# Holding K and V pools open across the dense phases of a decode step with gradients, with early V loads, fewer weight slabs and smaller K and V pools

## The chip, the cores and the metric

The kernel runs on one core of one Trainium2 chip. The metric is the time of one execution on the device in microseconds (us), as the median of several runs. A kernel that is compared is timed on the same chip, in the same rounds, as the kernel before. Ratios are the mean time of one kernel's fast runs over that of the other's fast runs of the same rounds, so they are not quite the ratio of the medians quoted beside them. Ratios are turned into microseconds with 2180 us.

## The reference, cut to what matters

Two layers of grouped-query attention over a cache of 65536 positions, and two feed-forward layers, for a single token, with all gradients. Both attention layers use the same K and V cache, and both feed-forward layers the same weights.

```python
def _A_ref(x, k_cache, v_cache, wq, wo):       # 32 query heads, 4 KV heads, head size 128
    q = (x @ wq)...
    scores = einsum("bhqd,bhkd->bhqk", q, k) * Dh ** -0.5
    o = einsum("bhqk,bhkd->bhqd", softmax(scores), v)
    return o... @ wo
x = A_x
x = x + _A_ref(_layernorm(x), ...)             # attention 1
x = x + _B_ref(_layernorm(x), w1, b1, w2, b2)  # relu(.)**2 in between
x = x + _A_ref(_layernorm(x), ...)             # attention 2
x = x + _B_ref(_layernorm(x), ...)
# outputs: x and its vjp: dx, dk_cache, dv_cache, dwq, dwo, dw1, db1, dw2, db2
```

## The kernel before

K and V are 67 MB each. They are read four times: by the two forward attentions, by a third pass that finds the query gradient of the second layer, and by a fourth pass that finds the rest and writes the gradients of both caches. Between the passes lie dense phases that read the weights. A border between a pass and a dense phase is called a seam below.

Every load goes through one queue, that of SP. A block of K or V is 512 KB, a weight slab 1 MB (896 KB of `w1`). Each attention opens its own pool of 8 K and 8 V blocks (4 and 4 in the fourth); each dense phase opens a pool of 6 slabs, and closes it at its end.

```python
KVBUFS = 8
...
@with_exitstack
def dense_phase(dctx, fn, resident_elems=0, wbufs=6):
    DENSE["w"] = dctx.enter_context(tc.tile_pool(name="wpool", bufs=wbufs))
    ...
    return fn()
...
class Stream:
    def block8(self, g, c8):
        ...
        if self.cur != (g, bb):
            self.t = ATT["kv"].tile([P, self.nblk, J, DH], BF, name=self.tag, tag=self.tag)
            self.eng.dma_start(out=self.t[:], in_=...)
        return self.t[:, bi, j:j + 8, :]
...
def attn_fwd(actx, qT, eT, lname):
    ...
    ATT["kv"] = actx.enter_context(tc.tile_pool(name=lname + "_kv", bufs=KVBUFS))
    ktpool = actx.enter_context(tc.tile_pool(name=lname + "_kt", bufs=5))
    spool = actx.enter_context(tc.tile_pool(name=lname + "_sp", bufs=2))
    ...
    # kT transposes K, kS forms scores; v8 (P times V) runs 78 items of 8 x 128 positions later
    pipeline(NI, [(kT, 0), (kS, TLEAD), (v8, TLEAD + IPG + LAG8)])
```

The last line gives each forward attention three stretches: one that reads K alone (the first 78 of 256 items), one where K and V alternate, and one that reads V alone (the last 78).

The row dots of the backward pass (`RowDots`, used by `mv_T`) multiply each row of a weight slab by a vector, shared out to DVE, ACT and PE. In the tail, `mv_T` over `wq` is interleaved with background tiles of the gradient of `wq` (`bg_per_block`).

## Time and profile before

| | before |
|---|---|
| time, median | 2180.55 us (2178.66 to 2184.33) |
| profiled span | 2176.8 us |
| bytes moved | 825.57 MB, mean 379 GB/s |

Lines of the page of the kernel before: the span, then the DMA row and the rate in 40 equal slices (9 is 90% or more busy), and the DMA total.

```profile
span 2176.8 us, 69255 instructions
DMA  8999999999999999699999987899999999999976
GB/s 350 388 407 408 406 398 358 401 353 390 407 407 405 390 365 392 250 407 408 407 406 404 388 340 245 316 415 405 353 417 418 393 409 393 407 410 416 412 291 235
DMA packets 229106, 825.57 MB, mean 379 GB/s; under 512 B 23748, under 2 KB 23748, under 8 KB 223684
```

The rate is 404 to 408 GB/s in the slices where the first three passes stream K and V steadily, up to 418 in the fourth, and lower at the seams. Next, the table of stretches of the kernel before, cut at the stages that the timeline of PE shows. The columns are the stretch in us, its length, busy time and count on PE, PE's weight load, DVE, ACT and POOL, the granted clock, the DMA share and GB/s. The lines are, in order: K alone in attention 1, K and V in attention 1, the dense phase between attentions 1 and 2, then K alone, K and V, and V alone in attention 2, the third attention, and the row dots before the fourth.

```profile
26.80:91.80 65.00, 56.01 (x1223) 54.74 (x1222) 39.77 (x68) 36.64 (x53) 0.00 (x0) 1.00 0.99 382
91.80:317.80 226.00, 192.59 (x4316) 177.41 (x4315) 96.41 (x162) 89.63 (x125) 0.00 (x0) 0.98 1.03 406
...
367.80:454.70 86.90, 45.87 (x1170) 43.40 (x1169) 24.91 (x68) 18.92 (x34) 0.00 (x0) 0.50 0.95 364
454.70:519.80 65.10, 58.20 (x1256) 57.01 (x1255) 42.38 (x72) 34.50 (x52) 0.00 (x0) 0.92 0.98 382
519.80:746.10 226.30, 190.80 (x4284) 173.55 (x4283) 95.26 (x161) 88.61 (x124) 0.00 (x0) 1.00 1.03 406
746.10:795.70 49.60, 36.83 (x631) 31.87 (x629) 2.25 (x10) 7.52 (x19) 0.00 (x0) 0.62 0.95 369
...
916.60:1254.40 337.80, 289.38 (x6184) 249.35 (x6184) 137.68 (x197) 111.84 (x111) 0.00 (x0) 0.98 1.01 400
1254.40:1366.40 112.00, 68.02 (x862) 59.58 (x862) 90.83 (x176) 79.21 (x97) 3.54 (x2) 0.54 0.78 283
```

The issues of the SP queue before, from its timeline (start, length from the first to the last of the group, tile, count):

```profile
431.70 13.94 SPq L268 DMA_DIRECT2D w_slab<-in_A_wq_dram  x5
454.78 51.84 SPq L401 DMA_DIRECT2D kblk<-in_A_k_cache_dram  x40
506.67 0.64 SPq L401 DMA_DIRECT2D vblk<-in_A_v_cache_dram  x1
...
795.68 1.49 SPq L268 DMA_DIRECT2D w_slab<-in_A_wo_dram  x3
...
916.00 2.95 SPq L401 DMA_DIRECT2D vblk<-in_A_v_cache_dram  x6
```

Each first load after a seam is issued only when the earlier pool is wholly free: K at 454.78 us when the last product with `wq` ends, `wo` at 795.68 us when the last V product ends, V at 916.00 us after the last row dot.

### The profile page before, as it was taken

The numbers are of one execution on the slowest core, as the hardware profiler recorded it, in microseconds if no ns is written. First come the engines' busy times: TensorE is split into PE (matmuls) and PEld (weight loads), VectorE is DVE, ScalarE is ACT, GpSimd is POOL, SyncE is SP. The second block draws the span as 40 slices with busy tenths as digits, with TensorE's granted clock in tenths as the row PEclk, the third lists the DMA queues.
The fourth block names the chain that finished last, engine by engine and source line by source line (L and its number), as shares of the span: only waits on it lengthen the run. The fifth ranks groups of instructions, "written<-read, shape, count | busy, mean of one in ns | idle before, by whom it ended". The sixth has DMA issues, their size and how long they took to land. (4 is left out here: it accounts for less than half of the span.)

```text
span 2176.8 us, 69255 instructions
## 1 busy us (share of the span) xinstructions
PE 1696.0 (78%) x30344; PEld 1332.2 (61%) x30344; DVE 1202.5 (55%) x2148; ACT 1002.1 (46%) x1532; POOL 280.4 (13%) x524
## 2 busy tenths in 40 slices
PE   5988876579888754688888866787887888788875
PEld 5978775578777744577777755444554444455542
DVE  4644430345434302744434478877877877776776
ACT  2543440235433300633333367566566566665644
POOL 0000000000000000000000000333433433443320
PEclk9999995579999955599999955899999999998976
DMA  8999999999999999699999987899999999999976
GB/s 350 388 407 408 406 398 358 401 353 390 407 407 405 390 365 392 250 407 408 407 406 404 388 340 245 316 415 405 353 417 418 393 409 393 407 410 416 412 291 235
DMA packets 229106, 825.57 MB, mean 379 GB/s; under 512 B 23748, under 2 KB 23748, under 8 KB 223684
## 3 DMA queue, kind: packets, MB, share of 16 engines
q1 hardware_dynamic: 184836, 655.46, 76.9%
q0 software_dynamic: 43968, 165.70, 18.9%
q8 instruction: 237, 3.88, 0.7%
q14 instruction: 65, 0.53, 0.1%
HBM read 655.37 MB, written 165.69 MB: 377 GB/s over the span
## 5 line engine op out<-in xcount | busy, mean ns | idle before, releaser
L175 DVE COPY kt<-ps_tr 128x1024 bf16<-128x1024 bf16 x482 | 331.4, 688 | 264.5 <-PE ps_tr L438 131.8
L172 ACT CAST gst<-ps_gg 128x512 bf16<-128x512 f32 x607 | 323.8, 593 | 187.1 <-PE ps_gg L768 139.7
L175 DVE CAST gst<-ps_gg 128x512 bf16<-128x512 f32 x417 | 273.2, 685 | 82.7 <-PE ps_gg L768 55.1
L172 ACT COPY kt<-ps_tr 128x1024 bf16<-128x1024 bf16 x158 | 159.8, 1012 | 307.7 <-PE ps_tr L438 143.0
L175 DVE COPY kt<-ps_gr 128x1024 bf16<-128x1024 bf16 x245 | 168.2, 687 | 164.7 <-PE ps_gr L438 90.6
L438 PEld LDWEIGHTS <-kblk 128*128 128x128 bf16 x4096 | 239.1, 99 | 16.8 <-issue 10.5
L457 PE MATMUL ps_sc<-L_qpad,kt 128*128 128x64 bf16 x4096 | 201.6, 195 | 57.1 <-DVE kt L175 48.6
L172 ACT COPY kt<-ps_gr 128x1024 bf16<-128x1024 bf16 x139 | 140.7, 1012 | 210.7 <-PE ps_gr L438 115.6
L768 PE MATMUL ps_gg<-GG,xt 64*128 64x512 bf16 x1024 | 193.2, 394 | 44.9 <-ACT og L172 19.1
L702 PEld LDWEIGHTS <-vblk 128*128 128x128 bf16 x2048 | 138.4, 101 | 138.0 <-issue 124.5
L501 PE MATMUL ps_acc<-eT,vblk 128*128 128x64 bf16 x4096 | 198.4, 206 | 24.0 <-DMA vblk<-in_A_v_cache_dram 22.5
L457 PEld LDWEIGHTS <-kt 128*128 128x128 bf16 x4096 | 159.3, 99 | 82.2 <-DVE kt L175 68.0
L501 PEld LDWEIGHTS <-vblk 128*128 128x128 bf16 x4096 | 169.7, 104 | 37.0 <-DMA vblk<-in_A_v_cache_dram 35.4
L702 PE MATMUL ps_tr<-ident_b,vblk 128*128 128x128 bf16 x2048 | 183.8, 227 | 6.5 <-ACT xt L172 5.8
L350 ACT ACTIVATE junka<-mvt_t 128x1024 bf16<-128x1024 bf16 (+2 forms) x88 | 139.9, 1590 | 96.1 <-DMA w_slab<-in_B_w_dram 59.3
L791 POOL MEMSET gw_ar<- 128x3584 bf16 (+1 forms) x2 | 4.1, 2052 | 1361.1 <-DVE mvt_t L349 1361.1
L438 PE MATMUL ps_tr<-ident_b,kblk 128*128 128x128 bf16 x2048 | 160.8, 222 | 12.7 <-DMA kblk<-in_A_k_cache_dram 9.3
L438 PE MATMUL ps_gr<-ident_b,kblk 128*128 128x128 bf16 x2048 | 159.7, 222 | 0.0
L603 PEld LDWEIGHTS <-vblk 128*128 128x128 bf16 x2048 | 118.1, 99 | 19.1 <-DMA vblk<-in_A_v_cache_dram 13.6
L762 PE MATMUL ps_acc<-X,kblk 128*128 128x64 bf16 x2048 | 118.9, 196 | 0.0
L172 ACT CAST og<-ps_gg 128x512 bf16<-128x512 f32 x139 | 81.1, 585 | 81.9 <-DMA out_dram<-og 44.1
L626 PE MATMUL ps_sc<-B_dOpad,kt 128*128 128x64 bf16 x2048 | 98.4, 195 | 26.0 <-DVE kt L175 19.9
(222 smaller groups left out, 2397.9 us busy)
## 6 DMA issues: line engine op xcount, KB each, us to landing
kblk<-in_A_k_cache_dram SPq DMA_DIRECT2D x512, 512.0 KB, 10.2
vblk<-in_A_v_cache_dram SPq DMA_DIRECT2D x512, 512.0 KB, 10.1
out_dram<-gst POOLq DMA_DIRECT2D x256, 512.0 KB, 10.5
w_slab<-in_A_wq_dram SPq DMA_DIRECT2D x32, 1024.0 KB, 8.2
w_slab<-in_A_wo_dram SPq DMA_DIRECT2D x32, 1024.0 KB, 12.7
w_slab<-in_B_w_dram SPq DMA_DIRECT2D x32, 896.0 KB, 8.3
w_slab<-in_B_w_dram SPq DMA_DIRECT2D x21, 1024.0 KB, 13.8
out_dram<-og POOLq DMA_DIRECT2D x60, 256.0 KB, 8.6
```

The source lines that it names most:

```text
L172: nc.scalar.copy(out=out, in_=in_)
L175: nc.vector.tensor_copy(out=out, in_=in_)
L350: nc.scalar.activation(out=self.junka[:, 0:N], in_=t[:, 0:N], func=ACTF.Copy, accum_out=self.y[:, kc:kc + 1])
L438: nc.tensor.transpose(pt[:, i, :], kb8[:, i, :], ident_b[:, :])
L457: nc.tensor.matmul(ps_s[:, slot:slot + 8, :].rearrange("p a b -> p (a b)"), lhsT=kt[:, i, :], rhs=qpad[:, g, :, :].rearrange("p a b -> p ( ...
L501: nc.tensor.matmul(ps_o[:, :, :].rearrange("p a b -> p (a b)"), lhsT=vb8[:, i, :], rhs=eT[:, g, :, c:c + 8], start=(c == 0), stop=(c == C ...
L603: nc.tensor.transpose(pt[:, i, :], vb8[:, i, :], ident_b[:, :])
L626: nc.tensor.matmul(ps_dp[:, slot:slot + 8, :].rearrange("p a b -> p (a b)"), lhsT=vt[:, i, :], rhs=dOpad[:, g, :, :].rearrange("p a b -> p ...
L702: nc.tensor.transpose(pt[:, i, :], vb8[:, i, :], ident_b[:, :])
L762: nc.tensor.matmul(ps_dq[:, :, :].rearrange("p a b -> p (a b)"), lhsT=kb8[:, i, :], rhs=X[:, sl:sl + 2, :].rearrange("p a b -> p (a b)"), ...
L768: nc.tensor.matmul(pgs[t2][:, :], lhsT=xt[64 * t2:64 * t2 + 64, blk0 + half, :], rhs=GG[64 * t2:64 * t2 + 64, :, :, :].rearrange("p a b c ...
L791: nc.gpsimd.memset(rows[:, 0:n], 0.0)
```

## The change

The intent: let loads cross the seams. For the first three attentions the K and V pool is opened before the dense phase, so the first blocks can be loaded while it runs. To make room, this pool has 4+4 instead of 8+8 buffers in the second and third attention (the fourth had 4+4 before), and the dense phases have 4 slabs instead of 6. In each forward attention up to six V blocks are asked for early, during the K-only stretch. The tail gets 8 instead of 4 background tiles per block. Arithmetic and traffic stay the same. The diff, with cuts:

```diff
+    VPRE = 6
+    KVBUFS_G = 4
...
-    def dense_phase(dctx, fn, resident_elems=0, wbufs=6):
+    def dense_phase(dctx, fn, resident_elems=0, wbufs=4):
...
+        def prefetch(self, g, bb):
+            ...
+            self.pre[(g, bb)] = self._load(g, bb)
...
-        ATT["kv"] = actx.enter_context(tc.tile_pool(name=lname + "_kv", bufs=KVBUFS))
+        assert ATT.get("kv") is not None
...
         def kT(idx):
             g, c8 = items[idx]
             kb8 = kstream.block8(g, c8)
+            if g == 0 and NPRE > 0:
+                step = max(1, (IPG - 8) // NPRE)
+                if idx % step == step - 1 and idx // step < NPRE:
+                    vstream.prefetch(0, idx // step)
...
+    kvs = open_kv("kv1", KVBUFS)
     L1 = dense_phase(lambda: attn_q(x0, "L1"))
     L1["oT"], L1["oTb"], L1["rZ"] = attn_fwd(L1["qT"], eT1, "L1")
+    kvs.close()
+    kvs = open_kv("kv2", KVBUFS_G)
...                                    # likewise kv3 (4+4) before the third attention
-            dn1 = mv_T(A_wq, D, QD, dqT1[:], "B1_dn", bgtasks=wq_tasks, bg_per_block=4)
+            dn1 = mv_T(A_wq, D, QD, dqT1[:], "B1_dn", bgtasks=wq_tasks, bg_per_block=8)
```

More of the change, by code (lines that the diff above doesn't have):

```diff
@@ L394, in __init__, with _load @@
             self.nblk = nblk
+        def _load(self, g, bb):
+            t = ATT["kv"].tile([P, self.nblk, J, DH], BF, name=self.tag, tag=self.tag)
+            self.eng.dma_start(out=t[:], in_=self.views[g][bb * self.nblk:(bb + 1) * self.nblk].rearrange("n p j d -> p n j d"))
+            return t
+        def prefetch(self, g, bb):
+            if not hasattr(self, "pre"):
+                self.pre = {}
+            self.pre[(g, bb)] = self._load(g, bb)
         def block8(self, g, c8):
@@ L399, in block8 @@
             if self.cur != (g, bb):
-                self.t = ATT["kv"].tile([P, self.nblk, J, DH], BF, name=self.tag, tag=self.tag)
-                self.eng.dma_start(out=self.t[:], in_=self.views[g][bb * self.nblk:(bb + 1) * self.nblk].rearrange("n p j d -> p n j d"))
+                pre = getattr(self, "pre", {})
+                if (g, bb) in pre:
+                    self.t = pre.pop((g, bb))
+                else:
+                    self.t = self._load(g, bb)
                 self.cur = (g, bb)
@@ L431, in attn_fwd @@
         state = {}
+        NPRE = min(VPRE, C // J)
         def kT(idx):
@@ L587, in attn_bwd3 @@
         state = {}
-        ATT["kv"] = ctx3.enter_context(tc.tile_pool(name=lname + "_kv", bufs=KVBUFS))
+        assert ATT.get("kv") is not None
         ktpool = ctx3.enter_context(tc.tile_pool(name=lname + "_kt", bufs=5))
@@ L659, in attn_bwd4 @@
         dqT = vec.tile([P, HQ], F32, name=lname + "_dqT")
-        ATT["kv"] = ctx4.enter_context(tc.tile_pool(name=lname + "_kv", bufs=4))
+        assert ATT.get("kv") is not None
         ktpool = ctx4.enter_context(tc.tile_pool(name=lname + "_kt", bufs=3))
@@ L820, in outer2_tasks, with open_kv @@
                 yield unit
+    def open_kv(name, bufs):
+        st = ExitStack()
+        ATT["kv"] = st.enter_context(tc.tile_pool(name=name, bufs=bufs))
+        return st
+    kvs = open_kv("kv1", KVBUFS)
     L1 = dense_phase(lambda: attn_q(x0, "L1"))
     L1["oT"], L1["oTb"], L1["rZ"] = attn_fwd(L1["qT"], eT1, "L1")
+    kvs.close()
+    kvs = open_kv("kv2", KVBUFS_G)
     def g12():
@@ L832 @@
     L3["oT"], L3["oTb"], L3["rZ"] = attn_fwd(L3["qT"], eT3, "L3")
+    kvs.close()
+    kvs = open_kv("kv3", KVBUFS_G)
     def g23():
@@ L842 @@
     dqT3 = attn_bwd3(L3, dOT3, nd23, eT3, "B3")
+    kvs.close()
     def g34():
@@ L882, in bg @@
                     t()
+        kvs = open_kv("kv4", 4)
         dqT1 = attn_bwd4(L1, L3, dOT1, dOT3, nd21, nd23, eT1, eT3, "B1", bg=(bg if BGON else None))
+        ATT["kv"] = None
+        kvs.close()
         for t in tasks:
```

## The prediction

> **What bounds the kernel now.** DMA. The page's DMA row stands at 9 in nearly all slices; the table of stretches shows 405-408 GB/s where K and V stream steadily, up to 418 in the last backward pass. 825.57 MB at 407 GB/s take about 2028 us; the span is 2176.8 us. (The Trainium skill, "DMA: Bandwidth & Descriptors", section Specifications, gives a fabric ceiling of 435 GB/s; the trace stays just below.) So about 148 us are lost where DMA is not full. By 5 us stretches, against 407 GB/s (my estimates): start of the first attention (15-30 us) 5; K-only start of either forward attention 2.5 each; first attention to dense (360-375) 6; dense to second attention (440-460) 7; second attention to dense (790-800) 5; dense to third attention (890-920) 19; dense before the fourth (1250-1375) 42; tail (2080 to the end) 38.
>
> At each seam the timeline shows the first load held until the whole earlier pool is free: K issued at 454.78 as the last wq matmul ends, landed 3.9 us later; wo at 795.68 after the last V matmul, landed 5.9 us later; V at 916.00 after the last row dot.
>
> **What the change does.** Arithmetic and traffic stay.
> - Gains. First seam: two K blocks ahead (2 x 1.29 us), and V prefetch fills the K-only stretch: 4 us. Second attention to dense: the first four wo slabs no longer wait for the V buffers, the 5 us hole closes. Dense to third attention: four V blocks are issued behind the last wo slab while DVE/ACT work: 4 x 1.29 = 5 us. Tail: twice the background tiles per row-dot block, so the 32 copies left over after dx0 (2155 us to the end) move into gaps of DVE and ACT: 5 us.
> - Losses. Six weight slabs become four. Dense to second attention: the 4 K blocks fetched early (5.1 us) only pay for the two wq slabs (5.1 us) fetched later: gain about 0. Other dense chains: -2. Second forward attention with 4+4 instead of 8+8 buffers: a lone 512 KB load takes about 3.7 us, plus 1.1 us held by PE is 4.8 us against 4 x 1.29 = 5.1 us per cycle, so the K-only and V-only stretches have almost no slack: -5. Third attention, also 4+4: -1; K/V interleaved has about 4 us of slack.
> - Untouched: first attention to dense (the new, smaller pool lies inside the old one), third attention to dense, the dense phase before the fourth attention, the fourth itself.
>
> Sum: 4+5+5+5-2-5-1 = 11 us, all on the DMA-bound path except the tail.
>
> **Predicted: 2169 us, 8 in 10 between 2152 and 2186.** Faster by over 2%: 4%; within 2%: 93%; slower by over 2%: 3%.
>
> **What would show each step.** In 5 us stretches: no hole below 300 GB/s at second attention to dense; the third attention's steady 407 GB/s some 5 us earlier, with 4 V blocks landed at its start; V issues among the K issues in the first 50 us of the forward passes; the second forward's K-only and V-only stretches a few per cent under 385 and 405 GB/s, the SP queue waiting for PE (buffer release); the tail about 5 us shorter.
>
> **What would make it wrong.** 4+4 buffers starving the second forward by 10-20 us; four slabs exposing every layernorm or broadcast chain; og stores (two buffers) stalling the denser tail; or more slack than thought, so that all losses vanish (about 2160).

## More of the kernel before

K and V together run at 406 GB/s; there DMA is the limit. K alone runs at 382 GB/s with PE busy for 58.20 of 65.10 us, 4 of which pass before the first K block lands; after that PE waits for no K block (the wait is shown with the result). So that stretch is paced by PE, and DMA keeps up.

## The result and the profile after

The changed kernel takes 2213.14 us (2211.28 to 2215.96, 7 runs) against 2180.55 us. The ratio is 1.0148, with a 95% interval of 1.0138 to 1.0158: about 32 us slower. The same lines of the page after the change:

```profile
span 2207.7 us, 69246 instructions
DMA  9999999999999999899999977799999999999976
GB/s 370 349 408 407 406 395 359 372 336 332 407 407 402 380 337 382 300 383 407 407 403 401 396 287 280 276 412 409 349 415 418 377 409 404 402 402 417 417 295 240
DMA packets 229107, 825.57 MB, mean 374 GB/s; under 512 B 23749, under 2 KB 23749, under 8 KB 223685
```

The bytes are the same. The row of shares does not show all of the loss: the tenth slice stands at 9 before and after, while its rate fell from 390 to 332 GB/s. So the share is not a measure of throughput here. The table of stretches after, same stages in the same order:

```profile
31.60:97.80 66.20, 56.93 (x1192) 54.10 (x1191) 38.81 (x68) 36.75 (x53) 0.00 (x0) 1.00 0.99 376
97.80:321.50 223.70, 188.79 (x4321) 175.64 (x4321) 96.31 (x162) 89.48 (x125) 0.00 (x0) 0.99 1.02 401
...
370.90:463.00 92.10, 46.16 (x1170) 43.56 (x1169) 24.81 (x68) 18.92 (x34) 0.00 (x0) 0.50 0.94 357
463.00:533.40 70.40, 60.80 (x1255) 57.37 (x1254) 42.56 (x72) 34.95 (x51) 0.00 (x0) 0.97 0.93 327
533.40:762.40 229.00, 194.69 (x4287) 175.83 (x4287) 95.38 (x161) 88.75 (x124) 0.00 (x0) 0.99 1.02 400
762.40:823.60 61.20, 38.80 (x629) 33.18 (x628) 2.24 (x9) 7.46 (x19) 0.00 (x0) 0.58 0.93 328
...
943.60:1275.90 332.30, 286.08 (x6142) 244.75 (x6140) 136.49 (x199) 110.96 (x111) 0.42 (x1) 1.00 1.01 399
1275.90:1392.10 116.20, 72.55 (x862) 60.86 (x862) 88.77 (x175) 79.21 (x97) 0.58 (x1) 0.50 0.76 272
```

V alone in attention 2 takes 61.20 instead of 49.60 us at 328 instead of 369 GB/s. K alone takes 70.40 instead of 65.10 us, although its first K blocks were on the chip when it began. The dense phase before it takes 92.10 instead of 86.90 us, the first product ends at 31.60 instead of 26.80 us. Only the third attention is shorter by more than profiles differ anyway (3 us). What PE waited for in K alone of attention 2, before and then after (us in total, times, longest):

```profile
PE ps_tr L438 <- DMA kblk<-in_A_k_cache_dram: 4.0, 1, 4.0
```

```profile
PE ps_tr L459 <- DMA kblk<-in_A_k_cache_dram: 6.5, 13, 1.7
```

The single wait for the first block has gone, and 13 waits in the midst of the stream have come. The SP queue after the change, from its timeline:

```profile
16.75 2.89 SPq L270 DMA_DIRECT2D w_slab<-in_A_wq_dram  x4
...
451.28 14.26 SPq L400 DMA_DIRECT2D kblk<-in_A_k_cache_dram  x5
...
817.27 15.91 SPq L270 DMA_DIRECT2D w_slab<-in_A_wo_dram  x7
...
930.81 12.35 SPq L400 DMA_DIRECT2D vblk<-in_A_v_cache_dram  x5
```

So the loads do cross the seams as intended: K at 451.28 us, before the product with `wq` ends at 463.0; `wo` at 817.27, before the last V product ends at 823.6; V at 930.81 (a first block even at 912.76), before the row dots end at about 943. The loss comes from elsewhere. The following table holds the length in us of each stage, from the first and last matmuls of each stage in the timelines of the profiled runs. The last four columns are experiments that are told below. Stages that a run leaves alone differ by up to 3 us between profiles, which were taken on several chips. The row dots end with the product of PE that closes them; after the change and in e8 the first transposes of attention 3 already run before that point.

| stage | before | changed | 4 slabs (e1) | 4+4 in attention 2 (e12) | V prefetch alone (e5) | hoisted, no cuts (e8) |
|---|---|---|---|---|---|---|
| to the end of the first product with wq | 26.8 | 31.6 | 31.7 | 27.1 | 26.6 | 27.1 |
| attention 1, K alone | 65.0 | 66.1 | 64.3 | 66.1 | 71.9 | 58.9 |
| attention 1, K and V | 225.9 | 223.7 | 226.0 | 225.5 | 221.7 | 228.8 |
| attention 1, V alone | 50.0 | 49.4 | 50.5 | 50.5 | 50.6 | 49.6 |
| dense, to the end of the next wq | 86.9 | 92.1 | 93.1 | 85.7 | 85.3 | 81.6 |
| attention 2, K alone | 65.1 | 70.4 | 65.0 | 72.5 | 70.2 | 60.7 |
| attention 2, K and V | 226.4 | 229.0 | 225.7 | 231.2 | 219.3 | 227.4 |
| attention 2, V alone | 49.5 | 61.3 | 50.4 | 62.0 | 49.6 | 50.7 |
| dense, forward and row dots | 120.9 | 120.0 | 123.7 | 120.9 | 121.1 | 117.3 |
| attention 3 | 337.8 | 332.3 | 338.0 | 337.7 | 338.0 | 331.4 |
| row dots before attention 4 | 112.0 | 116.2 | 115.9 | 112.8 | 112.5 | 113.0 |
| attention 4 | 729.1 | 733.5 | 733.4 | 731.7 | 730.8 | 731.9 |
| tail | 81.3 | 82.2 | 81.1 | 82.8 | 81.2 | 82.9 |

### The profile page after: what moved, and what is told of

Same layout as the page of the kernel before. It is cut to its first block, busy times and chain, and to the rows that moved or that the text cites. A ratio compares the mean times of both kernels' runs of the same rounds, so it can differ in the third digit from the quotient of the medians.

```text
span 2207.7 us, 69246 instructions
## 1 busy us (share of the span) xinstructions
PE 1715.2 (78%) x30344; PEld 1338.8 (61%) x30344; DVE 1202.5 (54%) x2148; ACT 1001.6 (45%) x1532; POOL 280.6 (13%) x524
## 5 line engine op out<-in xcount | busy, mean ns | idle before, releaser
L522 PE MATMUL ps_acc<-eT,vblk 128*128 128x64 bf16 x4096 | 203.8, 208 | 35.8 <-DMA vblk<-in_A_v_cache_dram 32.6
L756 POOL COPY X<-eT 128x200 bf16<-128x200 bf16 x88 | 46.6, 529 | 986.8 <-ACT junka L352 941.2
L359 PE MATMUL ps_tr<-ident_b,w_slab 128*128 128x128 bf16 x776 | 96.9, 308 | 30.4 <-DMA w_slab<-in_B_w_dram 12.3
```

The source lines that it names most:

```text
L359: nc.tensor.transpose(pt[:, i, :], slab[:, (g0 + i) * P:(g0 + i + 1) * P], ident_b[:, :])
L522: nc.tensor.matmul(ps_o[:, :, :].rearrange("p a b -> p (a b)"), lhsT=vb8[:, i, :], rhs=eT[:, g, :, c:c + 8], start=(c == 0), stop=(c == C ...
```

## The experiments

Each part of the change was first put alone into the kernel before. The theory (A) was that two cuts made to fit the pools, slabs and KV buffers, cost some 15 to 22 us each, and that early V loads and the denser tail are worth nothing. A letter stands for the same theory in all runs; the further rivals (C to F) are stated in the expectation where they first occur. The main rival (B) was the prediction's own view: the cuts are nearly free.

**e1, four slabs alone.**

```diff
-    def dense_phase(dctx, fn, resident_elems=0, wbufs=6):
+    def dense_phase(dctx, fn, resident_elems=0, wbufs=4):
```

> The kernel before with four weight slabs instead of six, nothing else. Theory A (the weight slabs are a main cause): the first wq product ends about 5 us later, the dense phase between the two forward attentions takes about 5 us longer, the one between second and third attention about 3 us, the row-dot phase before the fourth attention 6 to 10 us; in all 15 to 22 us slower. Rival B (the prediction): the slabs have slack, at most 3 us slower in all, and the loss lies in the KV buffers and in the prefetch.

Measured: 2200.76 us against 2179.16 us, ratio 1.0100 (1.0084 to 1.0115), about 22 us slower. A holds, B falls. The first product shows the mechanism. Below is the SP queue of the kernel before, then that of e1.

```profile
5.77 12.22 SPq L268 DMA_DIRECT2D w_slab<-in_A_wq_dram  x5
26.86 33.03 SPq L401 DMA_DIRECT2D kblk<-in_A_k_cache_dram  x27
```

```profile
5.78 13.99 SPq L268 DMA_DIRECT2D w_slab<-in_A_wq_dram  x5
31.70 3.73 SPq L401 DMA_DIRECT2D kblk<-in_A_k_cache_dram  x8
```

The product cannot start before 15.8 us, when the layernorm is done. Before, six of its eight slabs are issued by then and two wait for a freed slab (16.81 and 17.67 us). With four, four have to wait, from 16.88 us on. The product ends 4.9 us later, which is two slabs of 1 MB at 407 GB/s (2 x 2.6 us). The K-only stretch is paced by PE, so it starts later and ends later. The same happens at the next product with `wq` (93.1 against 86.9 us) and in the row dots (115.9 against 112.0): there PE waits 9.2 us for slabs of the feed-forward weights and 4.5 us for slabs of `wo`, for which it had no wait of note before. With 2.8 us in the dense phase before attention 3, some 18 of the 22 us are found in these stages.

**e10 and e9, five and eight slabs alone.** The same line, with 5 and 8.

> The kernel before with five weight slabs instead of six. Theory A (each slab less is one slab, about 2.5 us of data, that is not on the chip when a chain of small operations ends and the products or row dots could run): half the cost of four slabs, 8 to 13 us slower than before. Rival E (four is a threshold below which the loads cannot keep up): at most 3 us slower.

> The kernel before with eight weight slabs instead of six. Theory A: the curve goes on, 5 to 15 us faster than before: the first wq product no longer waits for a freed slab (it ends up to 5 us earlier), the one before the second attention likewise. Rival E (threshold): no gain, within 3 us.

Measured: five slabs 2187.67 us, ratio 1.0038 (1.0022 to 1.0055), about 8 us slower, as A said, and E (3 us at most) falls; eight slabs 2175.76 us, ratio 0.9986 (0.9967 to 1.0004), about 3 us faster, with an interval from 7 us faster to 1 us slower. The first product ends at 31.7, 28.8, 26.8 and 26.2 us with 4, 5, 6 and 8 slabs. So the curve is steep below six and nearly flat above, where the slabs of this product are all issued by 8.9 us; by our count (the first landed at 6.4 us, seven more at 2.6 us each, 1 us of PE) the rate of DMA is then the limit. A expected more of eight slabs: the first product ends 0.6 us earlier and not up to 5, and of the 5 to 15 us in all only the lower end lies in the interval.

**e2, e3 and e12: four V buffers, four K buffers, and both, in attention 2 alone.** The stream gets its own count of buffers (`L3` is attention 2 in the program; the shown line is that of e2):

```diff
-                self.t = ATT["kv"].tile([P, self.nblk, J, DH], BF, name=self.tag, tag=self.tag)
+                self.t = ATT["kv"].tile([P, self.nblk, J, DH], BF, name=self.tag, tag=self.tag, bufs=self.bufs)
...
-        vstream = Stream(Vv, "vblk", nc.sync, NBLK)
+        vstream = Stream(Vv, "vblk", nc.sync, NBLK, bufs=4 if lname == "L3" else None)
```

> The kernel before with 4 V buffers (8 K buffers stay) in the second forward attention alone. Theory A (a load in a queue takes about 5.2 us to land, so four buffers make a cycle of 6.3 us against 5.1 us of data): the stretch that reads V alone grows from 49.6 to about 61 us, the rest stays; 10 to 13 us slower in all. Rival B (the prediction, 3.7 us to land): at most 3 us slower.

> The kernel before with 4 K buffers (8 V buffers stay) in the second forward attention alone. Theory A: the stretch that reads K alone (first K transpose to first V product, 61.1 us before, 70.1 us after the change) grows by 5 to 9 us, the V-only stretch stays at 50 us; 5 to 9 us slower. Rival C: the K-only stretch grew after the change because prefetched V blocks stand in the queue in front of K, then this run is within 2 us of before.

> The kernel before with 4 K and 4 V buffers in the second forward attention alone, the two single cuts (12 and 16 us) together. Theory A (each stretch is limited by its own stream): the V-only stretch is 12 to 13 us longer, the K-only stretch 9, the interleaved one 3 to 6, so 22 to 30 us slower than before. Rival F: the two cuts share their cost (a slow K stretch leaves V time to run ahead), 16 us or less, which is less than the second forward lost after the change (20 us).

Measured: V 2191.63 us, ratio 1.0056 (1.0039 to 1.0073), about 12 us slower; K 2195.11 us, ratio 1.0071 (1.0056 to 1.0086), about 15 us slower; both 2205.85 us against 2181.62 us, ratio 1.0112 (1.0096 to 1.0129), about 24 us slower. The prediction's view (about 5 us for both) falls in all three, and so does F. V hits only the stretch that reads V alone (62.7 us in e2). K hits K alone (74.0 us in e3) and also K with V (232.6 us), which A had left out, so that K cost more than the 5 to 9 us of A. Both together reproduce what attention 2 lost after the change. C (early V blocks delay K) is out as the only cause, because K alone grows without any early V.

The reason can be read in the DMA view. The lines give issues, size and the median time in us from issue to landing, in most of the V-only stretch: the kernel before (8 V buffers), e2 (4), and the changed kernel (4).

```profile
vblk<-in_A_v_cache_dram SPq DMA_DIRECT2D x30, 512.0 KB, 9.1
```

```profile
vblk<-in_A_v_cache_dram SPq DMA_DIRECT2D x30, 512.0 KB, 5.5
```

```profile
vblk<-in_A_v_cache_dram SPq DMA_DIRECT2D x31, 512.0 KB, 5.1
```

The windows were 38, 49 and 47 us long, so a block took 1.27, 1.63 and 1.52 us. The trace resolves the landing of 7 or 8 of the loads in each window; they lie between 6.7 and 9.4 us with 8 buffers, and between 4.6 and 6.4 us with 4. With 8 buffers, 9.1 us at a block every 1.27 us means some seven loads in the queue (an estimate), so most of it is queueing. With 4, a load still takes over 5 us to land, not the 3.7 us of the prediction. PE then holds the buffer for about 1 us (16 products of one block take 1.04 us in this stretch). A buffer's round of some 6.3 us over 4 buffers gives 1.6 us a block, against 1.29 us of data. The waits of PE in about the same windows, before, in e2 and in the changed kernel, say the same (what waits for what, us in total, times, longest):

```profile
PE ps_acc L501 <- DMA vblk<-in_A_v_cache_dram: 6.7, 20, 0.6
```

```profile
PE ps_acc L502 <- DMA vblk<-in_A_v_cache_dram: 16.9, 25, 1.9
```

```profile
PE ps_acc L522 <- DMA vblk<-in_A_v_cache_dram: 14.4, 25, 1.5
```

And the table of stretches of e2 for the V-only stretch shows a DMA share of 0.89 at 308 GB/s, where before it was 0.95 at 369:

```profile
743.90:806.60 62.70, 38.96 (x629) 33.31 (x629) 2.25 (x9) 7.46 (x19) 0.00 (x0) 0.57 0.89 308
```

**e4, five V buffers in attention 2 alone.** As e2, with 5.

> The kernel before with 5 V buffers (8 K) in the second forward attention alone. Theory A (a cycle of about 6.3 us, landing 5.2 plus 1.1 held, divided by the buffers): 6.3 / 5 = 1.26 us a block, just under the 1.29 us of data, so nearly all of the 13 us that four buffers cost is gone; 0 to 4 us slower than before. Rival D: any cut of the buffers costs in proportion (landing time grows with the queue), then 5 buffers cost 6 us or more.

Measured: 2184.67 us against 2179.43 us, ratio 1.0022 (1.0007 to 1.0037), about 5 us slower, between the two theories (A 0 to 4 us, D 6 us or more); the interval, 1.5 to 8 us, reaches into both. Over half of the 12 us is gone by the means. The landing time with five is 5.3 us in the DMA view and the stretch takes 53.9 us. So five is still a little short for this stream; the round is longer than landing and holding alone by an amount that was not resolved.

**e5, the V prefetch alone,** with 8+8 buffers and six slabs.

```diff
+            if g == 0 and NPRE > 0:
+                step = max(1, (IPG - 8) // NPRE)
+                if idx % step == step - 1 and idx // step < NPRE:
+                    vstream.prefetch(0, idx // step)
```

> The kernel before with the V prefetch alone (six blocks, 8+8 buffers, six slabs). Theory A: worth nothing, -1 to +2 us, because without it 7 V blocks are already issued before the first V product (the buffers are full then anyway) and the K-only stretch is paced by TensorE. Rival B (the prediction): 5 us faster, as the V blocks fill DMA time that the K-only stretch leaves. Rival C: V blocks in front of K in the queue delay K, 3 us or more slower.

Measured: 2180.29 us against 2179.16 us, ratio 1.0004 (0.9989 to 1.0019). A holds, B falls; the 3 us of C lie within the interval (2 us faster to 4 us slower), but the stages of attention 1 and 2 together lose under 1 us. Counted in the trace before, 7 V blocks are already issued when the first V product of either forward attention starts (the first at 506.67 us, 13 us before it): the queue runs ahead by itself as soon as the K buffers are full. The early V blocks push K back (K alone 71.9 and 70.2 instead of 65.0 and 65.1 us), and the next stretch gives about the same time back (221.7 and 219.3 instead of 225.9 and 226.4 us; 12.0 us lost and 11.3 gained over both attentions).

**e6, the denser tail alone.**

```diff
-            dn1 = mv_T(A_wq, D, QD, dqT1[:], "B1_dn", bgtasks=wq_tasks, bg_per_block=4)
+            dn1 = mv_T(A_wq, D, QD, dqT1[:], "B1_dn", bgtasks=wq_tasks, bg_per_block=8)
```

> The kernel before with twice the background tiles per row-dot block in the tail, nothing else. Theory A: the tail is bound by the sum of the copies on DVE and ACT and by the order on these queues; the copies move from after the last layernorm to before it, and the last layernorm and the store of dx0 move to the end; 0, within 2 us. Rival B (the prediction): 5 us faster.

Measured: 2183.35 us against 2179.43 us, ratio 1.0015 (1.0000 to 1.0030), about 3 us slower; in the profiled run the tail takes 80.2 against 81.3 us. B falls. A's "0, within 2 us" holds for the profiled stage and is just missed by the timing; what the other 2 or 3 us are is open.

**e7, the changed kernel with one part undone:** attention 2 opens its own 8+8 pool inside.

```diff
-        assert ATT.get("kv") is not None
+        if lname == "L3":
+            ATT["kv"] = actx.enter_context(tc.tile_pool(name=lname + "_kv", bufs=KVBUFS))
...
-    kvs = open_kv("kv2", KVBUFS_G)
```

> The changed kernel, with one part undone: the second forward attention opens its own pool of 8+8 buffers inside, as before, and no longer a hoisted one of 4+4 (its first K blocks then wait for the dense phase again, and the next wo slabs for the V buffers). Theory A: the V-only stretch returns to 50 us (-12) and the K and interleaved stretches lose their 8 us, but the seams cost 4 us each again; 10 to 16 us faster than the changed kernel, 2197 to 2203 us. Rival B (the prediction: 4+4 costs 5 us, the seams gain 5): within 3 us of the changed kernel.

Measured: 2195.67 us, ratio to before 1.0067 (1.0052 to 1.0082). The changed kernel's ratio is 1.0148, so this undoes about 18 us of the 32. That is a little more than A expected (10 to 16), and B (3 us) falls. V alone is back to 48.3 us.

**e8, hoisting without the cuts.** Six slabs stay. Only the stream that is read first is hoisted: 7 K buffers before the forward attentions, 7 V before the third, 4 V before the fourth. The pool that is in use last is placed above the short-lived ones, so that the slabs of the next dense phase lie over pools that are free early. Small stores go to the POOL queue, and the pools between get more buffers (`kt`: 8 and 16 instead of 5). There is no V prefetch. Core of the diff to the kernel before:

```diff
-        ATT["kv"] = actx.enter_context(tc.tile_pool(name=lname + "_kv", bufs=KVBUFS))
-        ktpool = actx.enter_context(tc.tile_pool(name=lname + "_kt", bufs=5))
+        ktpool = actx.enter_context(tc.tile_pool(name=lname + "_kt", bufs=8))
         spool = actx.enter_context(tc.tile_pool(name=lname + "_sp", bufs=2))
+        ATT["vblk"] = actx.enter_context(tc.tile_pool(name=lname + "_v", bufs=KVBUFS))
...                                    # third attention: K pool last; fourth: K pool inside
+    hs = open_blk("kblk", "k1", 7)
     L1 = dense_phase(lambda: attn_q(x0, "L1"))
...
+    hs.close()
+    hs = open_blk("kblk", "k2", 7)    # then "vblk", "v3", 7 and "vblk", "v4", 4
```

> A version from the findings: six weight slabs and eight buffers stay; only that stream is hoisted which is read first (7 K buffers for the forward attentions, 7 V for the third, 4 V for the fourth), and the pool of the stream that is read last is put above the short-lived ones, so that the first weight slabs after an attention wait for pools that are free early; small stores go to the POOL queue. No V prefetch, tail as before. Theory A (the seams are worth 4 to 6 us each as soon as nothing is paid for them): first attention starts 4 us earlier, attention to dense -5 twice and -5 once more before the row dots, dense to attention -4, third attention -8, fourth -5; 25 to 35 us faster than before, 2145 to 2155 us. Rival: hoisting is worth little in itself, DMA time saved at a seam is lost again in the stretch after it; then at most 12 us faster.

Measured: 2158.95 us (2157.14 to 2163.14) against 2179.43 us, ratio 0.9902 (0.9885 to 0.9918), about 21 us faster than before. The seam after attention 1, in 5 us stretches, before and then in e8:

```profile
360.00:365.00 5.00, 3.20 (x62) 2.76 (x63) 0.00 (x0) 0.00 (x0) 0.00 (x0) 0.73 0.85 340
365.00:370.00 5.00, 2.39 (x39) 1.91 (x36) 0.35 (x2) 0.00 (x0) 0.00 (x0) 0.50 0.21 48
```

```profile
360.00:365.00 5.00, 3.59 (x58) 2.96 (x55) 0.35 (x2) 0.00 (x0) 0.00 (x0) 0.50 1.03 391
365.00:370.00 5.00, 2.03 (x64) 1.87 (x64) 0.00 (x0) 0.00 (x0) 0.00 (x0) 0.50 1.05 387
```

The hole of 48 GB/s is closed. By the stage table, the K-only stretches are 6.1 and 4.4 us shorter, the two dense phases 5.3 and 3.6 us, the third attention 6.4 us. The rival falls, but A's 25 to 35 us was too much as well: the row dots before the fourth attention and that attention gained nothing, and K with V in attention 1 gave 3 us back. Since e8 changes several things at once, what each of them earns was not separated.

**e11, seven slabs and five hoisted buffers.** As e8, with `wbufs=7`, 5 instead of 7 hoisted buffers before attentions 1 to 3, and larger pools between.

> The hoisted version with seven weight slabs and 5 instead of 7 hoisted K or V buffers (and more buffers in the pool between, so that the slabs still lie over pools that are free early). Theory A: a slab more is worth 3 to 8 us; five K buffers in the forward attentions cost up to 4 us; 2150 to 2160 us, that is 0 to 8 us faster than the version with six slabs. Rival: five K buffers in the K-only stretch cost more than the slab gives, 2160 us or more.

Measured: 2166.08 us, ratio 0.9938 (0.9918 to 0.9957), so slower than e8. Its rival holds: in the two forward attentions K alone and K with V together take 5.2 and 5.1 us longer than in e8, more than the seventh slab gives. Pools between were changed too, so that this cost is put down to the five hoisted buffers by argument only.

## Why the prediction was wrong, point by point

The prediction said 2169 us, about 11 us faster; the changed kernel is about 32 us slower. In microseconds, the parts measured alone add up to 22 (slabs) + 24 (4+4 in attention 2) + 1 (V prefetch) + 3 (tail) = 50 slower. The change as a whole is 32 slower, so, if the parts simply add, the crossing of the seams brought about 18. This remainder was not measured alone in that layout, and it includes the cost of 4+4 buffers in attention 3, which no run has alone either. It agrees with what the stages show: about 4 us less between the end of `wq` and the first K transpose of attention 2, 4.3 us less between attention 2 and the first product with `wo`, 5.5 us in attention 3, and about 4 us in attention 1 (K alone, and K with V, take 289.9 us together against 293.6 with the V prefetch alone). And e8, which crosses the seams without the cuts, is 21 us faster than before.

- "Six weight slabs become four ... gain about 0 ... Other dense chains: -2." This is the first step that failed. It measured -22 us (e1). The prediction did see that K loaded early replaces slabs loaded late, and counted bytes. But the K-only stretch is paced by PE, so bytes that arrive early hardly repay a PE that starts late: K with V of attention 1 ends at 317.8 us before, at 321.9 us in e1 and at 321.5 us in the changed kernel, which had K loaded early (and V too). The words "all on the DMA-bound path" were wrong for this stretch: 382 GB/s with PE busy nearly throughout.
- "... a lone 512 KB load takes about 3.7 us ... -5." This is the second. The mechanism was right (buffers round against data), the term was mis-sized. The first, lone K blocks of the kernel before do keep PE waiting for 3.6 and 4.0 us. But with three or four loads in flight a load took 5.1 to 5.5 us, not 3.7, which turned "almost no slack" into 24 us (e2, e3, e12). The Trainium skill, "DMA: Bandwidth & Descriptors", section "Anatomy of one DMA — SWDGE (gpsimd) path", fits 2.0 us plus bytes at 436 GB/s for the GpSimd path. For 512 KB this would be 3.2 us, an estimate from that page. These loads are issued by SP, and the measured 5.1 to 5.5 us decides.
- "K/V interleaved has about 4 us of slack" (written of the third attention; the sum took nothing for this stretch in the second): with four K buffers it took 6 us more in attention 2 (e3), and 3 us more after the change.
- "V prefetch fills the K-only stretch", a part of the 4 us at the first seam: worth 0 (e5). The queue had already fetched V ahead. The skill's advice on the same page, section "Rules for kernel authors", to issue a DMA early, was already met here.
- "Tail ... 5 us": no gain (e6).
- Right: the seam after attention 2 closes (1.6 instead of 5.9 us from the last V product to the first `wo` product), attention 3 is 5.5 us shorter even with 4+4 buffers, the seam after attention 1 is untouched. The list of what could go wrong did name both main causes: "4+4 buffers starving the second forward by 10-20 us" and "four slabs exposing every layernorm or broadcast chain". They were held to be exceptions, and both came true.

The two main losses are shown by runs that hold one cut alone and, for attention 2, by undoing it (e7); that the rest is the gain at the seams rests on adding up the parts. Attention 4 was 4 us longer in the changed kernel's profile and in e1's, but other runs that leave it alone lie up to 3 us above before too, so no cause is given for that.

## What to carry to other kernels

When a pool is hoisted so that loads can cross a seam, look at what was cut to make room: here each of the two cuts (22 and 24 us) cost more than all the crossed seams together gained (about 18 us, by the sum above). Count the round of a buffer with the landing time of a loaded queue, read from the trace in the very stretch, and not with that of a lone load. What worked here, as a whole (e8), was to hoist only the stream that is read first, and to place the pool that is freed last so that the next phase's loads do not lie over it.

## What the Trainium skill lacked or had wrong

- "DMA: Bandwidth & Descriptors": the fixed cost of about 2 us is given for DMAs issued by GpSimd. No figure for loads of this size in a moderately filled SP queue was found there; the runs show a median of 5.1 to 5.5 us for 512 KB with 4 or 5 buffers of the stream, and 9.1 us with 8. How many blocks a stream needs to be kept at its rate follows from that: V alone took 1.63 us (e2) and 1.52 us (changed kernel) a block with 4 buffers and 1.27 us with 8.
- Neither lacking nor wrong: "DMA: Bandwidth & Descriptors", section "Anatomy of one DMA — SWDGE (gpsimd) path", says that waits for semaphores are on the issuing sequencer and the DMA engines only consume their queues. The trace agrees where it was read: in e1 the slabs that wait for a free buffer are issued late by SP, from 16.88 us on. The fabric ceiling of 435 GB/s in its section "Specifications" was not reached by any slice of 54 us, of which the highest are 418 GB/s; a single 5 us stretch reads 437 GB/s (1260 to 1265 us of the kernel before), but the 15 us around it 398.
